# Rounding float64 weights on chip: the sign carried by a parametric activation on ScalarE in place of an operation on VectorE

## The chip, the cores and the metric

The kernel runs on one core of one Trainium2 chip. The metric is the time of one execution on the device in microseconds (us), the median of several runs. The profile is of one execution, with times counted from the start of its span. Its engines are PE (TensorE, matmuls; PEld is the loading of their weights), DVE (VectorE), ACT (ScalarE), POOL (GpSimd) and SP (SyncE, which here only issues transfers).

## The reference, cut to what matters

A retention block, linear attention with a decay per head, is followed by a SwiGLU feed-forward block. q, k and v are float32. The three weight matrices are float64, because `np.random.randn` gives float64 and nothing casts it.

```python
# attention: B, H, S, D = 8, 8, 576, 64
scores = scale * np.matmul(q, k.transpose(0, 1, 3, 2))
Dmat = np.where(rel >= 0, gamma[:, None, None] ** rel[None, :, :], 0.0)
attn = np.matmul(scores * Dmat[None], v).astype(np.float32)
x = attn.transpose(0, 2, 1, 3).reshape(B * S, H * D)          # 4608 x 512

# feed-forward: w_gate, w_val 512 x 1536, w_out 1536 x 512, all float64
g = x @ w_gate
silu = g * (1.0 / (1.0 + np.exp(-g)))
out = (silu * (x @ w_val) @ w_out).astype(np.float32)
```

[...]

## The kernel before: the parts that matter

The kernel works on the tokens in tiles. The first tile has 512 tokens and uses plain matmuls (`up0`, `down0`); while it runs, the weights arrive, are rounded, and sums of weight blocks are formed, which the later tiles of 1024 tokens use. Attention is woven in between: one `tick` moves three pairs of heads on by one stage each.

The weights come in 18 units of 1 MB, into a ring of three places. A unit has two halves of 128 x 512 numbers, and each half goes through `split` on ScalarE and then `rounding` on VectorE:

```python
def split(j):                                     # ScalarE
    i, f = halves[j]
    bits = bits_of(i, f)                          # 32-bit words of the float64 numbers: [..., 0] low, [..., 1] high
    top, ulp = [rest[:, part_at + 512 * (2 * n + j % 2) : ...] for n in range(2)]    # two places each, by j % 2
    nc.scalar.activation(out=blocks(top), in_=bits[:, :, :, 1].bitcast(F32), func=AF.Copy, scale=2.0 ** -112)
    nc.scalar.activation(out=blocks(ulp.bitcast(I32)), in_=bits[:, :, :, 0].bitcast(U32), func=AF.Copy, scale=2.0 ** -29)
    parts[j] = top.bitcast(I32), ulp.bitcast(I32)
    if f and j // 2 + RAWS < len(order):
        load_w(j // 2 + RAWS)                     # the next unit for this place of the ring

def rounding(j):                                  # VectorE
    i, f = halves[j]
    dst = weights[i][1][f].bitcast(I32)
    top, ulp = parts.pop(j)
    nc.vector.tensor_scalar(out=dst, in0=top, scalar1=3, scalar2=None, op0=ALU.logical_shift_left)       # L376
    nc.vector.scalar_tensor_tensor(out=top, in0=top, scalar=-(1 << 31), in1=dst,                         # L377
                                   op0=ALU.bitwise_and, op1=ALU.bitwise_or)
    nc.vector.tensor_tensor(out=dst, in0=top, in1=ulp, op=ALU.add)                                       # L379
    if j + 1 < len(halves):
        split(j + 1)
```

How this rounds: the high word of a float64 holds the sign, 11 bits of exponent and 20 of the fraction. Read as a float32, it has the sign, the upper 8 bits of that exponent in its own exponent field, and the other 3 bits, with the 20, in its fraction. The factor 2^-112 takes 112 from the exponent field. For the weights here what is left of the field is so small that a shift of the word by 3 to the left loses nothing of it, and the shifted word has just the exponent and the upper fraction of a float32. It does lose the sign, though, in bit 31; L377 takes that bit from `top` and puts it back. The low word, scaled by 2^-29 and rounded to an integer from 0 to 8, gives the last three bits of the fraction, and L379 adds it as an integer, with its carry.

The matmuls of the first tile:

```python
def up0(f, chunks):                               # f = 0 to 11
    pair = banks[2 * (f % 2) : 2 * (f % 2) + 2]   # bankA and bankB, or bankC and bankE
    for gv, bank in enumerate(pair):
        for c in chunks:
            nc.tensor.matmul(bank, w_up[...], xs[0][:, c, :], ...)                    # L567
    if HP - 1 in chunks:
        s = io[:, (f % 2) * T0 : (f % 2 + 1) * T0]
        nc.scalar.activation(out=s, in_=pair[0], func=AF.Silu)                        # L571
        nc.vector.tensor_tensor(out=hid0[f], in0=pair[1], in1=s, op=ALU.mult)         # L572, the product of f

down_order = [8, 9, 10, 0, 1, 11, 2, 3, 4, 5, 6, 7]
def down0(f):
    for i, bank in enumerate(banks):              # bankA, bankB, bankC, bankE
        nc.tensor.matmul(bank, hid0[f][:, ts(i, P)], w_dn[...], ...)                  # L579
```

The program of the first tile is one list, in which the halves to be rounded stand ahead of the matmuls that need them; each engine takes its instructions in that order. Other lines that the profile names:

- L403 to L414: transposes and scaling of q and k for attention (L410 on VectorE, L414 the scaling of keys on ScalarE)
- L426 to L462: attention's matmuls; L469 to L484: masks and states on VectorE, after ScalarE's copy `even` (L473); L511 and L513: attention's result into x
- L586: the first tile's output copied out of the banks
- L605: sums of blocks of x (VectorE), of weights and of hidden values (GpSimd, in part VectorE); L656: sums of `w_out` stored to memory, L283 to L290: the attention's loads, both on SP's queue
- L799 and L838: the matmuls of the later tiles; L740: sums of their results

Of the kernel before, what the change touches and what calls it, by code (L numbers as in the profile page):

```python
# [12 lines left out]
F32 = mybir.dt.float32  # L13
# [3 lines left out]
AF = mybir.ActivationFunctionType  # L17
ALU = mybir.AluOpType
# [131 lines left out]
def kernel(  # L150
# [32 lines left out]
    nc = tc.nc  # L183
# [21 lines left out]
    scale = 1.0 / math.sqrt(D)  # L205
# [131 lines left out]
    def load_w(m):  # L337
        i = order[m]
        raw = rest[:, raw_at + m % RAWS * 2048 : raw_at + (m % RAWS + 1) * 2048]
        raws[i] = raw.bitcast(I32)  # L340
        dst, src = raw.bitcast(I64), weights[i][0]
        if i < NUP:
            dst = dst.rearrange("p (c n) -> p c n", n=2 * P)
            for cols in (ts(0, P), ts(1, P)) if m == 0 else (slice(0, 2 * P),):
                nc.scalar.dma_start(out=dst[:, :, cols], in_=src[:, :, cols])
        else:
            nc.scalar.dma_start(out=dst.rearrange("p (f n) -> p f n", f=2), in_=src)

    def bits_of(i, f):

        if i < NUP:
            return raws[i].rearrange("p (c f m two) -> p f c m two", f=2, m=P, two=2)[:, f]
        return raws[i].rearrange("p (f c m two) -> p f c m two", f=2, m=P, two=2)[:, f]

    def split(j):

        i, f = halves[j]
        bits = bits_of(i, f)  # L360
        top, ulp = [rest[:, part_at + 512 * (2 * n + j % 2) : part_at + 512 * (2 * n + j % 2 + 1)] for n in range(2)]
        blocks = lambda a: a.rearrange("p (c m) -> p c m", m=P)
        nc.scalar.activation(out=blocks(top), in_=bits[:, :, :, 1].bitcast(F32), func=AF.Copy, scale=2.0 ** -112)
        nc.scalar.activation(out=blocks(ulp.bitcast(I32)), in_=bits[:, :, :, 0].bitcast(U32), func=AF.Copy, scale=2.0 ** -29)
        parts[j] = top.bitcast(I32), ulp.bitcast(I32)
        if f and j // 2 + RAWS < len(order):
            load_w(j // 2 + RAWS)

    def rounding(j):

        i, f = halves[j]
        dst = weights[i][1][f].bitcast(I32)
        top, ulp = parts.pop(j)
        nc.vector.tensor_scalar(out=dst, in0=top, scalar1=3, scalar2=None, op0=ALU.logical_shift_left)  # L376
        nc.vector.scalar_tensor_tensor(out=top, in0=top, scalar=-(1 << 31), in1=dst,  # L377
                                       op0=ALU.bitwise_and, op1=ALU.bitwise_or)
        nc.vector.tensor_tensor(out=dst, in0=top, in1=ulp, op=ALU.add)  # L379
        if j + 1 < len(halves):  # L380
            split(j + 1)

# [482 lines left out]
    for t in range(HP + 2):  # L865
        tick(t, 0, HP)
        if t == 2:
            split(0)
        if t in (2, 3, 4):
            for j in range(2):  # L870
                rounding(2 * (t - 2) + j)
        if t > 3:
            for f in range(2):
                up0(f, range(2) if t == 4 else range(2, HP))
# [14 lines left out]
    def round_until(i):  # L889
        while todo and order.index(i) >= todo[0]:  # L890
            m = todo.pop(0)
            plan.extend(lambda j=j: rounding(j) for j in (2 * m, 2 * m + 1))
# [92 lines left out]
```

## Time and profile before

| what | value |
|---|---|
| time, median of 3 runs | 1091.46 us (1091.33 to 1092.53) |
| span of the profiled execution | 1084.0 us |
| mean granted clock of TensorE | 0.994 |
| VectorE busy | 670.9 us, 62% |
| L376, shift: 36 instructions | 0.42 us each at the median |
| L377, sign: 36 instructions | 0.69 us each at the median |
| L379, add: 24 into `arena`, 12 into `rest` | 0.69 and 0.85 us each at the median |
| L363, ScalarE's Copy of the high words: 36 | 0.68 us each at the median |
| L364, ScalarE's Copy of the low words: 36 | 0.67 us each at the median |
| first and last instruction of the rounding | L363 at 27.5 us, L379 at 144.2 us |

How to read what follows. A row of the timeline has the start in us, the duration in us, engine, line, operation, output<-input with their shapes, the number of instructions, and in brackets how long the engine had been idle before and what released it. A row of groups has line, engine, operation, names and shapes and a count; then busy us and mean ns of one; then the idle time ahead of them. A row of stretches has the stretch from:to, its length, the busy us of each engine with the number of instructions, the granted clock of TensorE (1.00 is full), the mean busy share of the 16 DMA engines and GB/s. Some hundredths of overlap between instructions of one engine are usual[...].

### The profile page before, as it was taken

How to read it: one execution, taken by the hardware profiler on the slowest of the kernel's cores; microseconds unless marked ns; L12 is line 12 of the kernel's file. 1: busy time of each engine (PE TensorE's matmuls, PEld its weight loads, DVE VectorE, ACT ScalarE, POOL GpSimd, SP SyncE). 2: the span in 40 equal slices, each digit the busy share in tenths (PEclk: the TensorE clock that was granted, in tenths of full speed). 3: DMA queues.
4: the chain of work that ended last, by engine and by line, in shares of the span. 5: the costliest groups of instructions: out<-in, count | busy, mean ns of one | idle time of the engine just before them, and what ended most of it. 6: DMA issues, size and time to landing. Idle time of an engine off the chain costs nothing.

```text
span 1084.0 us, 21445 instructions
## 1 busy us (share of the span) xinstructions
PE 1047.0 (97%) x8420; PEld 859.6 (79%) x8420; DVE 670.9 (62%) x1063; ACT 267.5 (25%) x560; POOL 407.4 (38%) x357
## 2 busy tenths in 40 slices
PE   5899989999999899999999999999999999999998
PEld 4545445688888788888888888888888888888887
DVE  1699975976878867653646858535267464244644
ACT  3555511224232211222222111122211012231110
POOL 1002479566454403741216025622151375122504
PEclk9999999999999999999999999999999999999999
DMA  9989876656577878867657778554554555555653
GB/s 216 235 222 242 231 185 196 194 179 191 155 190 187 248 193 223 215 175 196 150 167 215 179 203 221 154 152 133 154 172 154 160 175 153 151 153 155 185 165 98
DMA packets 304212, 198.44 MB, mean 183 GB/s; under 512 B 219632, under 2 KB 247408, under 8 KB 304112
## 3 DMA queue, kind: packets, MB, share of 16 engines
q1 hardware_dynamic: 272512, 152.67, 54.3%
q10 hardware_dynamic: 31600, 44.41, 12.3%
q8 instruction: 67, 1.10, 0.4%
q14 instruction: 33, 0.27, 0.1%
HBM read 156.91 MB, written 40.11 MB: 182 GB/s over the span
## 4 chain that ended last, share of the span: by engine, by line
PE 79%; DVE 10%; DMA 4%; issue 3%; SPq 2%; POOL 2%; ACT 1%; ACTq 0%; DVEq 0%; POOLq 0%
PE bankA L799 11%; PE bankE L799 11%; PE bankB L799 11%; PE bankC L799 11%; PE bankE L838 6%; PE bankB L838 6%; PE bankC L838 6%; PE bankA L838 6%; PE outer L449 2%; DVE rest L740 2%; PE outer L426 1%; DVE rest L377 1%; DVE rest L605 1%; PE inner L462 1%; DMA v<-in_v_dram 1%
## 5 line engine op out<-in xcount | busy, mean ns | idle before, releaser
L740 POOL TENSOR_TENSOR rest<-rest 128x512 f32<-128x512 f32 x56 | 79.1, 1418 | 300.7 <-DVE rest L740 280.0
L814 ACT ACTIVATE io<-rest 128x256 f32<-128x256 f32 x180 | 75.0, 417 | 348.9 <-DVE rest L740 300.5
L799 PE MATMUL bankA<-rest,arena 128*128 128x256 f32 x544 | 130.5, 383 | 3.5 <-DVE rest L586 2.5
L799 PE MATMUL bankC<-rest,arena 128*128 128x256 f32 x544 | 129.3, 381 | 1.5 <-DVE rest L740 1.4
L605 POOL TENSOR_TENSOR rest<-rest 128x256 f32<-128x256 f32 (+1 forms) x86 | 83.6, 993 | 119.7 <-DVE rest L379 91.8
L605 POOL TENSOR_TENSOR arena<-arena 128x512 f32<-128x512 f32 (+1 forms) x72 | 115.2, 1614 | 32.6 <-DMA up<-arena 26.5
L799 PE MATMUL bankB<-rest,arena 128*128 128x256 f32 x512 | 121.9, 381 | 0.9 <-DVE arena L817 0.8
L799 PE MATMUL bankE<-rest,arena 128*128 128x256 f32 x512 | 121.4, 380 | 0.1
L799 PEld LDWEIGHTS bankA<-rest,arena 128*128 128x128 f32 x544 | 103.6, 191 | 19.8 <-issue 5.0
L799 PEld LDWEIGHTS bankC<-rest,arena 128*128 128x128 f32 x544 | 102.8, 190 | 16.8 <-issue 2.6
L821 POOL TENSOR_TENSOR arena<-rest,io 128x256 f32<-128x256 f32 x72 | 51.8, 726 | 168.8 <-ACT io L814 168.8
L799 PEld LDWEIGHTS bankB<-rest,arena 128*128 128x128 f32 x512 | 97.3, 191 | 15.4 <-DVE arena L817 1.2
L799 PEld LDWEIGHTS bankE<-rest,arena 128*128 128x128 f32 x512 | 96.9, 190 | 13.7 <-issue 0.4
L740 DVE TENSOR_TENSOR rest<-bankC,rest 128x512 f32<-128x512 f32 x72 | 48.9, 688 | 68.9 <-PE bankC L799 46.7
L740 DVE TENSOR_TENSOR rest<-bankE,rest 128x512 f32<-128x512 f32 x72 | 48.8, 686 | 67.5 <-PE bankE L799 49.3
L740 DVE TENSOR_TENSOR rest<-bankA,rest 128x512 f32<-128x512 f32 x72 | 48.8, 686 | 65.4 <-PE bankA L799 48.0
L740 DVE TENSOR_TENSOR rest<-bankB,rest 128x512 f32<-128x512 f32 x72 | 48.9, 687 | 62.6 <-PE bankB L799 46.3
L817 DVE SCALAR_TENSOR_TENSOR arena<-rest,io 128x256 f32<-128x256 f32 x84 | 53.8, 645 | 12.6 <-ACT io L814 12.6
L838 PE MATMUL bankB<-arena 128*128 128x256 f32 x252 | 58.2, 381 | 0.0
L838 PE MATMUL bankA<-arena 128*128 128x256 f32 x252 | 58.1, 380 | 0.0
L838 PE MATMUL bankC<-arena 128*128 128x256 f32 x252 | 58.0, 380 | 0.0
L838 PE MATMUL bankE<-arena 128*128 128x256 f32 x252 | 57.9, 380 | 0.0
(150 smaller groups left out, 1648.5 us busy)
## 6 DMA issues: line engine op xcount, KB each, us to landing
arena<-up SPq DMA_DIRECT2D x234, 256.0 KB, 2.7
arena<-dn SPq DMA_DIRECT2D x104, 384.0 KB, 3.6
up<-arena ACTq DMA_DIRECT2D x78, 256.0 KB, 2.8
out_dram<-rest SPq DMA_DIRECT2D x32, 256.0 KB, 3.3
qk<-in_q_dram SPq DMA_DIRECT2D x112, 72.0 KB, 3.3
qk<-in_k_dram SPq DMA_DIRECT2D x112, 72.0 KB, 2.9
v<-in_v_dram SPq DMA_DIRECT2D x62, 128.0 KB, 3.1
kn<-in_k_dram SPq DMA_DIRECT2D x58, 128.0 KB, 2.9
```

Source lines behind the costliest of these rows:

```text
L377: nc.vector.scalar_tensor_tensor(out=top, in0=top, scalar=-(1 << 31), in1=dst, op0=ALU.bitwise_and, op1=ALU.bitwise_or)
L426: m = nc.tensor.matmul(xo[half[hl], c, r], s["v"][half[r], c, hl, :], ret[half[r], hl, c], start=(c == 0), stop=(c == 0), skip_group_check ...
L449: nc.tensor.matmul(xr[half[hl]] if c + 1 == NC else xo[half[hl], c // 2, c % 2], state[half[hl], c, :], s["qT"][half[hl], ts(c, L)], start ...
L462: nc.tensor.matmul(sc[half[r], hl, c], kT[half[hl], at], qT[half[hl], at], start=True, stop=True, skip_group_check=True)
L605: eng.tensor_tensor(out=dst, in0=srcs[0], in1=srcs[1], op=ALU.add if op[0] == "add" else ALU.subtract)
L740: eng.tensor_tensor(out=at(op[1]), in0=at(op[2]), in1=at(op[3]), op=ALU.add if op[0] == "add" else ALU.subtract)
L799: nc.tensor.matmul(b[:, gv * TB : (gv + 1) * TB], w[:, gv, ts(c, P)], rhs[:, c, :], start=(opens and gv == 0 and c == 0), stop=(c == 1), s ...
L814: nc.scalar.activation(out=s, in_=src[:, 0:TB], func=AF.Silu, scale=-1.0 if negative else 1.0)
L817: return lambda: nc.vector.scalar_tensor_tensor(out=dst, in0=src[:, TB : 2 * TB], scalar=-1.0, in1=s, op0=ALU.mult, op1=ALU.mult)
L821: nc.gpsimd.tensor_tensor(out=dst, in0=src[:, TB : 2 * TB], in1=s, op=ALU.mult)
L838: nc.tensor.matmul(b[:, m * TB : (m + 1) * TB], lhs[:, qd, ts(m, P)], w[:, qd], start=(opens and qd == 0 and m == 0), stop=(qd == NQ - 1), ...
```

## The change

What is computed stays the same. The high word's activation becomes a parametric one: it multiplies by `scale` as before, and values below zero also by `alpha`, 2^32. That adds 32 to the exponent field of negative numbers, which is bit 28 of the word; the shift by 3 takes this bit to bit 31, where the sign belongs. VectorE's operation that put the sign back (L377) is then not needed, and the add works on the shifted word in place. Its aim is less work for VectorE.

```diff
-        nc.scalar.activation(out=blocks(top), in_=bits[:, :, :, 1].bitcast(F32), func=AF.Copy, scale=2.0 ** -112)
+        nc.scalar.activation(out=blocks(top), in_=bits[:, :, :, 1].bitcast(F32), func=AF.Prelu, scale=2.0 ** -112, alpha=2.0 ** 32)
         nc.scalar.activation(out=blocks(ulp.bitcast(I32)), in_=bits[:, :, :, 0].bitcast(U32), func=AF.Copy, scale=2.0 ** -29)
...
         nc.vector.tensor_scalar(out=dst, in0=top, scalar1=3, scalar2=None, op0=ALU.logical_shift_left)
-        nc.vector.scalar_tensor_tensor(out=top, in0=top, scalar=-(1 << 31), in1=dst,
-                                       op0=ALU.bitwise_and, op1=ALU.bitwise_or)
-        nc.vector.tensor_tensor(out=dst, in0=top, in1=ulp, op=ALU.add)
+        nc.vector.tensor_tensor(out=dst, in0=dst, in1=ulp, op=ALU.add)
```

## The prediction

> **What bounds the kernel now.** The page's first part comes first. It makes TensorE the bound of the whole span:
>
> ```profile
> PE 1047.0 (97%) x8420; PEld 859.6 (79%) x8420; DVE 670.9 (62%) x1063; ACT 267.5 (25%) x560; POOL 407.4 (38%) x357
> ```
>
> Such a share is an average, so I next placed the removed line in time. L377 runs 36 times, from 28.7 to 144.1 us, and nowhere later. So I cut the span at the places where the work changes and asked for busy times in those stretches. The columns are stretch, length, then busy us and instructions of PE, PEld, DVE, ACT and POOL, then clock, DMA share and GB/s.
>
> ```profile
> 26.00:37.00 11.00, 7.94 (x263) 7.50 (x263) 9.40 (x23) 7.02 (x15) 0.00 (x0) 0.85 1.01 242
> 37.00:116.00 79.00, 78.81 (x602) 38.43 (x590) 67.11 (x127) 39.77 (x71) 7.04 (x7) 1.00 0.96 232
> 116.00:151.00 35.00, 28.77 (x319) 15.13 (x320) 32.60 (x52) 13.45 (x26) 18.94 (x21) 0.95 0.73 198
> 151.00:187.00 36.00, 35.82 (x535) 20.38 (x534) 17.27 (x36) 3.98 (x9) 34.85 (x49) 1.00 0.69 201
> 187.00:205.00 18.00, 15.52 (x41) 8.70 (x40) 17.80 (x22) 1.68 (x4) 10.39 (x9) 0.91 0.49 149
> ```
>
> Most of the rounding lies in 37 to 116, and there TensorE is idle for 0.2 us of 79 at full clock. A faster VectorE can win nothing in it directly. From 116 to 151 it is the other way round: VectorE is busy 93% of the stretch, TensorE is idle for 6.23 us. The timeline of TensorE names these waits (the bracket is idle time before the row and its releaser):
>
> ```profile
> 117.16 3.70 PE L567 MATMUL bankA<-rest,arena 128*128 128x512 f32 x8 [1.18 <-ACT io L571]
> 135.50 0.69 PE L426 MATMUL outer<-ret,v 64*64 64x64 f32 x32 [1.10 <-DVE ret_last L477]
> 138.15 1.15 PE L449 MATMUL outer<-qT,state 64*64 64x64 f32 x32 [1.26 <-DVE state L484]
> 139.50 0.27 PE L456 MATMUL outer<-qT,kT 64*64 64x64 f32 x2 [0.20 <-DVE kT L410]
> 145.51 2.08 PE L579 MATMUL bankE<-rest,arena 128*128 128x512 f32 x2 [2.44 <-DVE arena L572]
> 147.38 1.77 PE L579 MATMUL bankA<-rest,arena 128*128 128x512 f32 x2
> ```
>
> The reader is to see that five waits add up to 6.18 us and that all come from a late VectorE. The first names ScalarE, but its SiLU at 116.52 stands behind two splits (115.40, 115.97) which had waited for VectorE's rounding. And the last wait leaves the clock low: two groups of L579 start 1.87 and 1.60 us apart, against 0.86 later, 1.75 us lost.
>
> How late VectorE is, its own timeline shows:
>
> ```profile
> 128.12 0.68 DVE L572 TENSOR_TENSOR arena<-bankE,io 128x512 f32<-128x512 f32 x1
> 144.77 0.68 DVE L572 TENSOR_TENSOR arena<-bankE,io 128x512 f32<-128x512 f32 x1
> ```
>
> These are the products of f = 9 and f = 11. TensorE had finished their bankE at 116.0 and 134.4, so VectorE is 12 and 10 us behind, without idle time of its own.
>
> [...] The trace [...] shows Copy, 0.66 us, and SiLU, 0.59 us, of 512 elements each close together; no run before has a Prelu. [...] L377 takes 0.69 us alone and up to 1.11 us while GpSimd is busy. [...] here a wait of 2.44 us was enough for a slow stretch, one of 1.26 us was not.
>
> **The change part by part.** The groups by form of VectorE from 28 to 145 us give the prices (busy us, mean ns, idle before):
>
> ```profile
> L379 DVE CUSTOM_DVE_ANT_0 arena<-rest 128x1024 uint16<-128x1024 uint16 x24 | 17.7, 738 | 2.3
> L377 DVE SCALAR_TENSOR_TENSOR rest<-rest,arena 128x512 int32<-128x512 int32 x24 | 16.7, 695 | 0.8
> L377 DVE SCALAR_TENSOR_TENSOR rest<-rest 128x512 int32<-128x512 int32 x12 | 10.4, 863 | 0.4
> L376 DVE TENSOR_SCALAR arena<-rest 128x512 int32<-128x512 int32 x24 | 10.1, 422 | 0.7 <-ACT rest L363 0.7
> ```
>
> *Removed:* 36 instructions of L377, 16.7 + 10.4 = 27.1 us of VectorE, and 0.03 us of gap each, 28 us in all. Of this, 25 of the 36 fall into 37 to 116, beside a dense TensorE.
>
> *Added:* nothing by count. The order of instructions on all five engines is otherwise the same, and both programs have two table loads[...]. I take Prelu at Copy's 0.68 us.
>
> *Moved:* the add reads the shifted word in place and now waits for the shift itself. `top` is free after the shift, one instruction earlier than before; ScalarE's second activation gets a wait of its own for the buffer of `ulp`, released by the add.
>
> *The new pace of a half.* Before, a half comes every 1.79 or 1.89 us when nothing disturbs (54.52, 56.31, 58.20). Less 0.73 (0.69 and the start gap), that is 1.06 to 1.16. ScalarE's two activations start 0.59 and 0.58 apart: 1.17 us a half. So both engines run at about 1.17, ScalarE just the slower: a gain of about 0.65 a half inside a run of halves.
>
> *Replay of VectorE.* I kept the order and let each product wait for its bank. From 91.2: four halves to 95.9, product f = 6, two halves, f = 7 at 100 (its bankE is full at 99.3), the attention pieces to 106.6, four halves to 111.3, f = 8 at 111.9 (117.49 before), four halves, f = 9 at about 117 (128.12 before). The backlog is gone, and from there the products follow the banks. f = 11 comes just after TensorE ends it.
>
> *Replay of TensorE.* It stays dense from 37 on. Without the five waits it reaches L579's first bank at 136.2 instead of 140.2 and then runs through: 6.18 us of waits and 1.75 us of low clock, 7.9 us.
>
> *Ahead of 37:* the wait of 2.68 us at 34.0 for L477 stands behind ScalarE's copy `even` (32.69), and ScalarE there is held by its copies and a DMA issue, not by L377. I give 0.1 us.
>
> *After 151:* TensorE is dense to 196.9, so all that follows should move ahead by the same 8 us. Sum: 8.0 us. I put 0.5 more for the stretch at 187 to 205 (below): 1091.5 - 8.5 = 1083.0.
>
> **The rivals.** (1) *All of VectorE's time returns*: 28 us off, 1063. The chain that ended last speaks for it, as it runs over L377 from 91 to 143; against it, TensorE is dense beside the first 25 of the 36. Unlikely. (2) *Transfers take the place of the wait.* The weights come as 1 MB loads in a ring of three, 5.7 to 6.8 us to land, and DMA is at 0.96 in 37 to 116. If VectorE gets ahead, the loads of the fifth and third last pair may come 1 or 2 us late. For it: little headroom. Against: nearly no split waited for weights before, and the replay has several us of slack ahead of each product's use. If it bites, the gain is 3 to 5: 1087. (3) *GpSimd does not move along.* Its sums are dense from 150.4 to 197.5, after stores queued behind the attention's loads. If these loads stay where they are, TensorE meets the sums at 199 earlier than GpSimd is ready, and 3 to 6 us come back: 1087. For moving along: the load ahead of those stores was issued at 139.47, right as VectorE's transpose ended at 139.38, so it comes forward with VectorE. (4) *More than 8.* From 187 to 199 VectorE's additions take 1.1 to 1.75 us instead of 0.69 beside GpSimd, and TensorE waits 2.48 us for the copy of bankA, then runs slowly (1.75 us). If GpSimd is done sooner, up to 4 more: 1079. (5) *Prelu dearer than Copy*: each 0.1 us would add 3.6 us to ScalarE, which is busy half of the time; nearly harmless.
>
> **Range and chances.** The waits of 6.2 us are named one by one and I trust them. The low clock, the stretch at 187 to 205, and (2) and (3) add about 4 us to either side: 1079 to 1088.5. A gain of 2% would need 21.8 us, of which only rival 1 is capable; a loss of 2% would need an effect that neither the order nor the trace shows.
>
> **What the profile after must show.** 36 fewer VectorE instructions, its busy time near 644; Prelu at 0.66 to 0.70 us; two table loads. TensorE idle under 1 us from 116 to 145, the first L579 near 136, no slow pair there; the product of f = 9 near 117. The first L799 near 191.5. The prediction is wrong if TensorE's idle time comes back with a DMA or GpSimd as releaser, if Prelu costs clearly more, or if the low clock shows up elsewhere.

## The result, and the profile after

Measured side by side, the kernel before took 1091.39 us and the changed one 1086.33 us (medians of four runs each). The ratio is 0.9956 with a 95% interval of 0.9937 to 0.9976, about 5 us or 0.4% less. A second comparison of the same two programs, with 22 and 51 runs, gave 0.9992 (0.9979 to 1.0006), which is no difference. Executions of either program are spread over some 8 to 10 us (the 51 runs of before from 1085.2 to 1093.2), so a few runs decide little here. The two intervals, put in us, are a gain of 2.6 to 6.9 and of -0.7 to 2.3; they don't overlap, so I claim no more than a gain between nothing and 5 us, where 8.5 had been predicted. For the mechanism I rely on the traces, and on experiments that moved the time by 11 to 14 us.

The first part of the page of after, in the form of the row shown of before:

```profile
PE 1046.6 (96%) x8420; PEld 861.8 (79%) x8420; DVE 642.2 (59%) x1027; ACT 267.4 (25%) x560; POOL 402.0 (37%) x357
```

VectorE has 36 instructions and 28.7 us of work less, and TensorE's share has not grown. Where VectorE's time went, the same stretches tell (stretch, length, then busy us and instructions of PE, PEld, DVE, ACT and POOL, then clock, DMA share, GB/s), here of after:

```profile
26.00:37.00 11.00, 6.48 (x218) 5.85 (x209) 7.62 (x20) 7.55 (x16) 0.00 (x0) 0.91 0.97 239
37.00:116.00 79.00, 78.82 (x618) 39.54 (x616) 53.52 (x107) 41.71 (x74) 5.95 (x7) 0.99 0.96 241
116.00:151.00 35.00, 35.00 (x470) 19.36 (x470) 20.73 (x40) 10.95 (x21) 16.03 (x21) 1.00 0.72 182
151.00:187.00 36.00, 30.45 (x388) 17.44 (x387) 16.64 (x33) 3.98 (x9) 34.84 (x49) 0.91 0.68 200
187.00:205.00 18.00, 15.44 (x50) 8.99 (x49) 17.79 (x22) 2.08 (x5) 10.28 (x9) 1.00 0.49 152
```

From 116 to 151 TensorE is busy for 35.00 of 35 us, where it had been for 28.77: the stretch that the change was meant for is repaired, and its clock is at 1.00. But from 151 to 187, which was dense before, TensorE is now busy for 30.45 of 36 us at a clock of 0.91. What was won in the one stretch is lost in the next. The rows with a wait in TensorE's timeline from 130 to 200 us name the waits (idle time before the row and its releaser in brackets):

```profile
156.64 0.70 PE L425 MATMUL outer<-ret,v 64*64 64x64 f32 x32 [3.13 <-DVE ret_last L476]
160.25 1.97 PE L448 MATMUL outer<-qT,state 64*64 64x64 f32 x32 [2.24 <-DVE state L483]
185.14 0.33 PE L444 MATMUL outer<-ret_last,vl 64*64 64x64 f32 x4 [0.18 <-PE outer L425]
199.46 1.97 PE L798 MATMUL bankA<-rest,arena 128*128 128x256 f32 x8 [2.56 <-DVE rest L585]
```

(Behind the rounding a line of after has a number one lower than the same line of before; L363, L364 and L376 of before, the splits and the shift, are L364, L365 and L377 of after, and its L378 is the add.) Between 130 and 153 us there is no wait at all. The last group of L578 ahead of the two waits comes 8.00 us before the same group of the kernel before (after, then before):

```profile
152.49 1.02 PE L578 MATMUL bankE<-rest,arena 128*128 128x512 f32 x2
```

```profile
160.49 1.02 PE L579 MATMUL bankE<-rest,arena 128*128 128x512 f32 x2
```

Then attention's matmuls wait 3.13 and 2.24 us for VectorE's masks and states, and at 164.94 the lead is down to 0.18 us (the same group of before starts at 165.12). The later tiles' first matmul, L798, begins at 199.46. Before it began at 199.57:

```profile
199.57 3.27 PE L799 MATMUL bankA<-rest,arena 128*128 128x256 f32 x8 [2.48 <-DVE rest L586]
```

VectorE isn't late of itself now. Its own timeline and that of ScalarE, both of after, lead on to the cause:

```profile
155.77 0.69 DVE L468 TENSOR_TENSOR ret<-inner,near 128x512 f32<-128x512 f32 x1 [8.86 <-ACT even L472]
```

```profile
153.53 1.71 ACTq L655 DMA_DIRECT2D dn<-rest  x3
155.36 0.37 ACT L472 COPY even<-inner 128x256 f32<-128x256 f32 x1 [17.42 <-DMA dn<-rest]
165.88 0.37 ACT L472 COPY even<-inner 128x256 f32<-128x256 f32 x1 [9.34 <-DMA dn<-rest]
```

The mask L468 waits 8.86 us for ScalarE's copy `even`. TensorE had finished the copy's input at 146.4, but ScalarE reaches it only after three stores of `w_out` sums (L655) that stand ahead of it in its order. The third row is the next tick's. The chain of waits that ended last runs over the same places: GpSimd's sums at 150.36 and 153.47, ScalarE's store at 154.22, `even` at 155.36, L468 at 155.77, the state at 159.23, and TensorE's L448 at 160.25.

ScalarE issues 24 of the 78 stores of these sums; not all are on SP's queue, as the list of lines said. The other 54 and attention's loads share the queue of SP, of which these are some rows in after:

```profile
113.88 11.63 SPq L655 DMA_DIRECT2D dn<-rest  x9
125.61 2.08 SPq L283 DMA_DIRECT2D qk<-in_q_dram  x4
133.88 5.48 SPq L655 DMA_DIRECT2D dn<-rest  x9
139.45 2.09 SPq L283 DMA_DIRECT2D qk<-in_q_dram  x4
147.83 3.96 SPq L655 DMA_DIRECT2D dn<-rest  x8
```

and the same queue in before, where these three rows answer to the last three:

```profile
133.69 5.43 SPq L656 DMA_DIRECT2D dn<-rest  x9
139.47 2.76 SPq L283 DMA_DIRECT2D qk<-in_q_dram  x4
147.91 3.96 SPq L656 DMA_DIRECT2D dn<-rest  x8
```

The starts agree within 0.2 us, although VectorE was 10 us behind in the one kernel and not in the other. So close an agreement is in part chance: in second executions, described below, the three rows start at 135.84, 141.60 and 150.56 (before) and at 133.97, 140.19 and 149.22 (after). But neither execution of after has them some 8 us earlier, so from here on this chain of sums, stores and loads doesn't follow the rounding. In before it couldn't be seen. There the copy `even` came at nearly the same time, after ScalarE had been idle for 14.20 us, and TensorE had nothing to wait for because it reached the tick's first matmul only at 161.44 (timeline of ScalarE in before):

```profile
155.79 0.38 ACT L473 COPY even<-inner 128x256 f32<-128x256 f32 x1 [14.20 <-POOL rest L605]
```

GpSimd, at last, waits for the stores to free the places of its sums (timeline of GpSimd in after):

```profile
117.65 1.88 POOL L604 TENSOR_TENSOR rest<-rest 128x256 f32<-128x256 f32 x2 [16.95 <-DMA dn<-rest]
135.92 0.72 POOL L604 TENSOR_TENSOR rest<-rest 128x256 f32<-128x256 f32 x1 [6.38 <-DMA dn<-rest]
150.36 1.40 POOL L604 TENSOR_TENSOR rest<-rest 128x256 f32<-128x256 f32 x2 [6.98 <-DMA dn<-rest]
196.27 1.17 POOL L604 TENSOR_TENSOR rest<-rest 128x256 f32<-128x256 f32 x1
```

A store waits for a sum, a sum waits for an earlier store, and the loads of attention stand between them in the same queue. The last of these sums ends at 197.4 in after and at 197.6 in before, and the later tiles' first matmul follows about 2 us behind it. It isn't released by GpSimd, though, but by VectorE's copy L585 at 198.63, which stands behind VectorE's own sums of x. These begin at 187.24 (187.43 in before), right after attention's last result, and take up to 1.75 us each beside GpSimd, where the ones after 198 take 0.69.

### The profile page after: what moved, and what is told of

Read it like the earlier page. It is cut to its first block, busy times and chain, and to the rows that moved or that the text cites. A ratio compares the mean times of both kernels' runs of the same rounds, so it can differ in the third digit from the quotient of the medians.

```text
span 1084.9 us, 21409 instructions
## 1 busy us (share of the span) xinstructions
PE 1046.6 (96%) x8420; PEld 861.8 (79%) x8420; DVE 642.2 (59%) x1027; ACT 267.4 (25%) x560; POOL 402.0 (37%) x357
## 4 chain that ended last, share of the span: by engine, by line
PE 82%; DVE 8%; DMA 4%; issue 2%; POOL 2%; SPq 1%; ACT 1%; ACTq 0%; DVEq 0%; POOLq 0%
PE bankE L798 10%; PE bankC L798 10%; PE bankA L798 10%; PE bankB L798 10%; PE bankE L837 6%; PE bankB L837 6%; PE bankA L837 6%; PE bankC L837 6%; PE outer L448 3%; PE bankA L566 2%; PE bankC L566 2%; DVE rest L739 2%; PE bankE L566 2%; PE bankB L566 2%; DVE rest L604 2%
## 5 line engine op out<-in xcount | busy, mean ns | idle before, releaser
L798 PE MATMUL bankA<-rest,arena 128*128 128x256 f32 x544 | 129.1, 380 | 3.6 <-DVE rest L585 2.6
L798 PE MATMUL bankC<-rest,arena 128*128 128x256 f32 x544 | 129.3, 381 | 2.5 <-DVE rest L739 1.4
L604 POOL TENSOR_TENSOR rest<-rest 128x256 f32<-128x256 f32 (+1 forms) x86 | 80.6, 958 | 124.7 <-DMA kn<-in_k_dram 89.5
L798 PE MATMUL bankE<-rest,arena 128*128 128x256 f32 x512 | 122.8, 383 | 0.0
L798 PE MATMUL bankB<-rest,arena 128*128 128x256 f32 x512 | 121.9, 381 | 0.9 <-DVE arena L816 0.8
L798 PEld LDWEIGHTS bankA<-rest,arena 128*128 128x128 f32 x544 | 103.1, 190 | 19.2 <-issue 5.0
L798 PEld LDWEIGHTS bankC<-rest,arena 128*128 128x128 f32 x544 | 102.9, 190 | 17.8 <-issue 2.6
L798 PEld LDWEIGHTS bankB<-rest,arena 128*128 128x128 f32 x512 | 97.5, 191 | 15.2 <-DVE arena L816 1.2
L798 PEld LDWEIGHTS bankE<-rest,arena 128*128 128x128 f32 x512 | 97.8, 192 | 14.0 <-DVE rest L739 0.4
```

Source lines behind the costliest of these rows:

```text
L604: eng.tensor_tensor(out=dst, in0=srcs[0], in1=srcs[1], op=ALU.add if op[0] == "add" else ALU.subtract)
L798: nc.tensor.matmul(b[:, gv * TB : (gv + 1) * TB], w[:, gv, ts(c, P)], rhs[:, c, :], start=(opens and gv == 0 and c == 0), stop=(c == 1), s ...
```

## The experiments

The theory to be tested: **a second limit stood right behind the first**, namely the sums on GpSimd together with their stores in the queues of SP and ScalarE, and it didn't move with VectorE. Rivals: the parametric activation costs something; the whole difference is chance between executions; the waits at 156 and 160 come only from ScalarE's order, without GpSimd; attention's transfers are late by themselves. Each kernel was compared with the kernel before on the same chip, and ratios are to that kernel.

| kernel | median us | ratio (95%) |
|---|---|---|
| c1_control: before, unchanged | 1091.10 | 1.0002 (0.9987 to 1.0017) |
| c4_prelu_only: before, with Prelu, sign kept | 1090.65 | 1.0003 (0.9989 to 1.0017) |
| c2_after_free: after, `even` and keys on VectorE | 1092.36 | 1.0012 (0.9996 to 1.0028) |
| c3_before_free: before, the same move | 1092.01 | 1.0024 (1.0011 to 1.0038) |
| d1_after_again: after, unchanged | 1089.06 | 0.9992 (0.9979 to 1.0006) |
| d2_after_ready: after, stores wait for no sum | 1074.77 | 0.9870 (0.9852 to 0.9888) |
| d3_before_ready: before, the same | 1087.93 | 0.9994 (0.9981 to 1.0007) |
| d4_after_first: after, first nine stores on ScalarE | 1086.28 | 0.9980 (0.9969 to 0.9991) |
| e1_after_even: after, only `even` on VectorE | 1089.04 | 0.9997 (0.9983 to 1.0011) |
| e2_after_first_even: the last two together | 1086.78 | 0.9972 (0.9960 to 0.9985) |
| e3_after_acts_even: all 26 stores on ScalarE, and `even` | 1083.71 | 0.9939 (0.9917 to 0.9961) |
| e4_after_pool: after, the 26 stores issued by GpSimd | 1078.08 | 0.9894 (0.9874 to 0.9913) |

### How much is chance

**c1_control** is the kernel before, with no edit.

> The kernel before, unchanged, as a control and for a second profile of it. Theory A (the 8 us won at 116 to 151 us are real, and most of them are given back from 151 to 163 us, where ScalarE's copy `even` stands behind stores that wait for GpSimd): ratio 1.000 +- 0.002; the second profile again shows TensorE idle for about 6 us between 116 and 151 us and dense from 151 to 187. Rival C (the first profile of before, at a span of 1084.0 us, was a short execution, and only the tail after 199 us differs between executions): the first L799 again at about 199.5, and the rest longer by some us.

The ratio is 1.0002. Its profile again has five waits from 116 to 151 us, 6.07 us in all (four of them in the same places as before; the fifth, 0.49 us, is at bankB instead of attention's L426), and L799 begins at 198.51, but then TensorE waits five times between 205 and 221 us, 3.7 us in all, which the first profile of before doesn't show. The profile of before was of a short execution (span 1084.0, against 1086.2 in the control; by the metric 1085.71 us, 5.8 below the median of its runs). Part of what the spans of single profiles differ by comes from there, so I compare starts ahead of 200 us rather than spans.

**d1_after_again** is the changed kernel, with no edit.

> The changed kernel once more, for a firmer ratio and a second profile. All theories: ratio 0.996 +- 0.002; TensorE dense from 116 to about 153, then waits of some 5 us between 153 and 163.

The ratio is 0.9992. TensorE is busy for 35.00 of 35 us from 116 to 151 again, and the waits after it are larger than in the first profile of after (timeline of TensorE):

```profile
158.13 1.13 PE L425 MATMUL outer<-ret,v 64*64 64x64 f32 x32 [5.21 <-DVE ret_last L476]
200.84 3.59 PE L798 MATMUL bankA<-rest,arena 128*128 128x256 f32 x8 [2.19 <-DVE rest L585]
```

Here L798 begins 1.3 us later than in before, and its first group takes 3.59 us after the wait. The same group took 3.27 us in before, at a granted clock of 0.58, and 1.97 us in after, at 1.00. Both executions show the stretch repaired and its gain gone by 200 us.

### Does Prelu cost anything

**c4_prelu_only** takes the new activation into the kernel before and keeps the operation for the sign:

```diff
-        nc.scalar.activation(out=blocks(top), ..., func=AF.Copy, scale=2.0 ** -112)
+        nc.scalar.activation(out=blocks(top), ..., func=AF.Prelu, scale=2.0 ** -112, alpha=2.0 ** 32)
```

> The kernel before with Prelu in place of Copy, and the sign operation kept (the result is the same). All theories: Prelu costs ScalarE what Copy does (0.67 us), VectorE is as late as before; ratio 1.000 +- 0.002. If Prelu had a cost of its own, 36 of them would show as more than 2 us.

The ratio is 1.0003: nothing. The instruction itself took 0.674 us at the median in after, Copy 0.682 in before, and ScalarE is busy for 267.8 us of the first 1084 in this run, where it was for 267.5 in before. This rival is out.

### A first attempt at the second limit, and a mistake

**c2_after_free** and **c3_before_free** let VectorE do the copy `even` and the scaling of keys in ticks 10 to 12, so that no attention work stands behind the stores on ScalarE:

```diff
         def keys():
             for hl in range(2):
+                if 10 <= i <= 12:
+                    nc.vector.tensor_scalar(out=kn[:, :, hl, :], in0=kn[:, :, hl, :], scalar1=key[...], scalar2=None, op0=ALU.mult)
+                    continue
...
-            nc.scalar.copy(out=even, in_=z[:, 0])
+            if 10 <= i + 1 <= 12:
+                nc.vector.tensor_copy(out=even, in_=z[:, 0])
+            else:
+                nc.scalar.copy(out=even, in_=z[:, 0])
```

> The changed kernel, and for the ticks 10 to 12 the copy `even` and the scaling of keys are on VectorE in place of ScalarE, whose queue holds the stores of GpSimd's sums. Theory A: the two waits of TensorE at 156.6 (3.13 us) and 160.3 (2.24 us) and the slow clock behind them are gone, TensorE is dense from 116 to about 189, the first L798 comes near 192 to 194 in place of 199.5, and the time falls by a further 4 to 7 us against the changed kernel: near 1080, ratio to before about 0.989. Rival B (attention's load number 10, or the sums themselves, are what is late, and not ScalarE's order): TensorE waits at 153 to 160 as before, now for VectorE which waits for a transfer; time as the changed kernel, 1086. Rival D (what is won ahead of 199 is given back at 199 to 220, where TensorE meets GpSimd's sums too early): dense to 189, but then waits for GpSimd of about the same size; 1086.

> The kernel before with the same move of ticks 10 to 12 to VectorE. Theory A: VectorE's backlog up to 145 us is the limit there and ScalarE's order is not, so nothing is gained: ratio 1.000 +- 0.002, or 1 us slower by the extra work on VectorE. If the move alone is worth 4 us or more here, theory A is wrong on the two limits standing one behind the other.

Neither is faster: the ratios are 1.0012 and 1.0024. Theory A's 1080 us for the first is far off, and the second is some 2.6 us slower, a little more than expected. The copy no longer waits for a store, but the scaling of keys took a wait with it into VectorE's order (timelines of VectorE, TensorE and SP's queue in c2_after_free):

```profile
175.89 0.54 DVE L414 TENSOR_SCALAR kn<-kn,tab 128x256 f32<-128x256 f32 x1 [19.04 <-DMA kn<-in_k_dram]
```

```profile
178.73 1.14 PE L429 MATMUL outer<-ret,v 64*64 64x64 f32 x32 [11.89 <-DVE ret_last L483]
```

```profile
171.82 1.13 SPq L264 DMA_DIRECT2D kn<-in_k_dram  x2
```

The keys' load is issued only at 171.82 (166.65 in after). Ahead of it in SP's queue stand eight loads of q and k, which waited 15.7 us in all for earlier stores of sums. VectorE stood still for the keys for 19 us, with all that followed. So the run doesn't test what I meant it to. It does show that SP's queue is late as well, not only ScalarE's order.

### Taking the wait for the sums away

**d2_after_ready** and **d3_before_ready** leave GpSimd's sums in place, but let each store of a `w_out` sum read a block that has long been rounded. The stores have the same size, queue and order, and wait for no sum; no sum waits for a store to have read its place, either. The later tiles compute with other weights because of this, so the kernel computes something else there; the amount of work is the same.

```diff
                 src, queue = view(slot), nc.scalar if late else nc.sync
+                src = w_dn[:, qd, 0, 0]
```

> The changed kernel; every store of a sum of w_out takes its data from a block that was rounded long ago in place of GpSimd's sum (the same bytes from the same queues in the same order; the later tiles then compute with other weights). So no store waits for GpSimd, and no sum waits for a store to have read its place. Theory A2 (the chain of GpSimd's sums, their stores in SP's and ScalarE's queues, and the attention's loads and ScalarE's work that stand behind these stores, runs at its own pace and ends the stretch from 153 to 187): TensorE dense from 116 to about 188, the first L799 near 190 to 194 in place of 199.5, time 5 to 8 us below the changed kernel: 1079 to 1081. Rival B2 (attention's transfers themselves are late, whatever stands ahead of them): waits of TensorE for masks or keys of 4 us or more remain between 150 and 180, time as the changed kernel.

> The kernel before with the same stores of ready data. Theory A2: VectorE's backlog still ends the stretch up to 145, the first L579 stays near 140 with the waits of 6 us ahead of 146; 151 to 187 was dense already, so the gain is at most what contention at 187 to 205 gives, 0 to 4 us: 1087 to 1091. A gain of 5 us or more here would mean that the stores and not VectorE's sign operation were the limit of the kernel before.

With the change, this takes 1074.77 us, a ratio of 0.987; without it, 1087.93 us, a ratio of 0.9994. This is the clearest result, and the gain is larger than theory A2's 5 to 8 us. Neither the change nor ready stores alone is worth a measurable gain in these runs (0.9992 and 0.9994), but both together are worth 1.3%, about 14 us. The stretches from 151 on in d2_after_ready:

```profile
151.00:187.00 36.00, 35.82 (x406) 19.13 (x405) 19.17 (x35) 2.81 (x6) 16.79 (x20) 1.00 0.85 238
187.00:205.00 18.00, 17.90 (x81) 15.11 (x80) 17.55 (x24) 6.59 (x13) 8.71 (x6) 1.00 0.88 247
```

TensorE is dense through both, and its first matmul of the later tiles begins 11.85 us earlier than in after (timeline of TensorE, then of ScalarE):

```profile
187.61 1.89 PE L799 MATMUL bankA<-rest,arena 128*128 128x256 f32 x8
```

```profile
145.24 0.37 ACT L472 COPY even<-inner 128x256 f32<-128x256 f32 x1 [8.61 <-PE inner L461]
```

The copy `even`, at 155.36 in after, no longer waits for a store but for TensorE. Attention's loads hardly started earlier: in after those at 125.61, 139.45 and 151.89, here at 124.13, 139.36 and 153.93; only the last one's keys left clearly earlier, at 161.12 and not 166.65. So the second limit lies in what waits for a sum or a store, not in the start of these loads, and this is against rival B2.

In d3_before_ready the first limit is still there, and late VectorE makes TensorE wait as late as 152.93 us:

```profile
124.87 5.82 PE L567 MATMUL bankA<-rest,arena 128*128 128x512 f32 x8 [5.68 <-ACT io L571]
152.93 1.97 PE L579 MATMUL bankE<-rest,arena 128*128 128x512 f32 x2 [2.57 <-DVE arena L572]
```

The wait at 124.87 was 1.18 us in before: its SiLU stands behind splits that wait for VectorE. So the edit also made VectorE later, and the 0.9994 isn't the worth of ready stores with the first limit left as it was. VectorE works beside a busier GpSimd there (27.4 us from 116 to 151, against 18.9 in before), and its 47 instructions of that stretch take 33.46 us, where 52 took 32.60 in before; that this is the reason wasn't tried. The wait ahead of the later tiles' first matmul, 2.48 us in before, is gone in this run; that matmul comes at 204.39.

### Which queue has to be relieved

Five more kernels keep all the arithmetic and change only where a store is issued, or where `even` is copied.

**d4_after_first** lets ScalarE issue the first nine of the 26 stores, which come after f = 7:

```diff
-                plan.append(lambda ..., late=f + 1 == NF: group(late))
+                plan.append(lambda ..., late=f in (7, NF - 1): group(late))
```

> The changed kernel, with the first nine stores of sums (those of f = 7) issued by ScalarE in place of SP, where they stand behind the attention's load 8 and GpSimd waits 17 us for them (100.7 to 117.7). The result is the same. Theory A2: GpSimd's sums, the stores after them and the loads 9 to 11 all come forward by 5 to 10 us, the waits of TensorE at 153 to 163 shrink or go, time 3 to 7 us below the changed kernel: 1080 to 1083. Rival B2: the loads are paced by the weights' transfers up to 120 us and come forward little; 1086. Rival E: ScalarE's splits now wait behind the stores, VectorE gets late again; 1087 to 1090.

The ratio is 0.998. The waits at 155 and 159 are 1.53 and 2.25 us (3.13 and 2.24 in after), and L798 begins at 198.01, 1.5 us earlier than in after: a small part of the loss, and less than the 3 to 7 us expected (the changed kernel had 0.9992 in this comparison). Only the first of the three loads came forward much, from 125.61 to 114.94; the others came 3.6 and 1.6 us earlier.

**e1_after_even** moves only `even` to VectorE, as in c2, and leaves the keys on ScalarE.

> The changed kernel, with the copy `even` of ticks 10 to 12 on VectorE and the scaling of keys left on ScalarE. The result is the same. Theory A3 (after d2: the stores that wait for GpSimd's sums hold both ScalarE's `even` and, in SP's queue, the attention's load 11): the waits of TensorE near 156 for the masks shrink to under 2 us, but the keys of tick 11, loaded late, stop it near 170 by some us; first L799 near 197 to 199, time 0 to 3 us below the changed kernel. Rival F (only ScalarE's order holds TensorE): TensorE dense to 189, time 6 us or more below the changed kernel.

The ratio is 0.9997. The wait for the masks is gone, and the keys take its place, since they stand behind the same stores (TensorE, then ScalarE):

```profile
156.85 1.42 PE L434 MATMUL inner<-v,kn 64*64 64x64 f32 x29 [4.70 <-ACT kn L413]
```

```profile
156.29 0.51 ACT L413 ACTIVATE kn<-kn,tab 128x256 f32<-128x256 f32 x1 [20.33 <-DMA dn<-rest]
```

So moving single pieces of work out of ScalarE's order didn't help here. This is against the rival that held ScalarE's order alone responsible.

**e2_after_first_even** has both edits.

> The changed kernel with both: `even` of ticks 10 to 12 on VectorE, and the first nine stores issued by ScalarE. The result is the same. Theory A3: sums and load 11 some us earlier, so 3 to 6 us below the changed kernel, ratio to before 0.994 to 0.997. Rival F: no more than e1.

The ratio is 0.9972, about 3 us. The later tiles begin at 192.84, 6.6 us earlier than in after. But the three stores of the output that stand ahead of ScalarE's part of the first tile's output (L590) then take 6.22 us to issue, against 1.62 in after; L590 comes at 201.58, released by a store of a sum, and TensorE waits for it (timeline of TensorE):

```profile
202.31 3.61 PE L801 MATMUL bankE<-rest,arena 128*128 128x256 f32 x8 [4.05 <-ACT rest L590]
```

**e3_after_acts_even** has all 26 of these stores on ScalarE, with `even` on VectorE, so that SP's queue holds only loads there:

```diff
-                plan.append(lambda group=groups.pop(0)[1], late=f + 1 == NF: group(late))
+                plan.append(lambda group=groups.pop(0)[1]: group(True))
```

> As e2, but all stores of the sums of the first quarter of w_out (26) are issued by ScalarE, so that SP's queue has only the attention's loads up to load 11. The result is the same. Theory A3: loads 9 to 11 come forward by 5 us or more; if ScalarE's splits don't fall behind, 4 to 8 us below the changed kernel. Rival E (ScalarE's splits and SiLU fall behind the stores): TensorE waits for ScalarE between 100 and 140, time as the changed kernel or above.

The ratio is 0.9939. TensorE is dense from 151 to 205 us, but ahead of that ScalarE stands for 14.74 us behind eleven stores before a split of weights at 127.60; the SiLU that follows begins only at 132.90, and TensorE waits for it, as rival E had it (timeline of TensorE):

```profile
133.53 6.29 PE L569 MATMUL bankC<-rest,arena 128*128 128x512 f32 x8 [7.80 <-ACT io L573]
```

**e4_after_pool** lets GpSimd issue the 26 stores itself, right after the sums that they store. No other engine then stands behind one of these 26 sums; the stores of later sums stay on SP and ScalarE.

```diff
-                src, queue = view(slot), nc.scalar if late else nc.sync
+                src, queue = view(slot), nc.gpsimd if qd == 0 else nc.scalar if late else nc.sync
```

> The changed kernel, with those 26 stores issued by GpSimd itself. The result is the same. Theory A3: no queue of another engine waits for these sums, SP's loads 9 to 11 come forward, TensorE's waits at 153 to 163 shrink; each issue costs GpSimd time, and [...] its sums end 0 to 10 us later or earlier than at 197; time 1 to 6 us below the changed kernel. Rival G (GpSimd's time for the issues exceeds what its waits were): sums end after 205, TensorE waits for them there, time above the changed kernel.

It takes 1078.08 us, a ratio of 0.9894 (0.9874 to 0.9913), 11.2 us less than before, and more than the 1 to 6 us below the changed kernel that were expected. The changed kernel wasn't part of this comparison; its own ratios were 0.9956 and 0.9992. Its six runs lie within 1.6 us. Its stretches:

```profile
116.00:151.00 35.00, 34.88 (x469) 19.10 (x468) 30.29 (x52) 14.15 (x28) 31.22 (x45) 1.00 0.78 210
151.00:187.00 36.00, 35.82 (x406) 19.14 (x405) 19.86 (x34) 2.81 (x6) 34.03 (x44) 1.00 0.65 190
```

TensorE is dense in both. GpSimd is busy for 31.2 us of the first, of which 9.65 us are the issuing of 17 stores; so 21.6 us are work on sums, where it had been 16.0. From 99 to 152 us its longest wait for a store to free a place is 0.73 us, against 16.95 in after. Its last sum and TensorE's start of the later tiles come 10.7 and 8.7 us earlier than in after:

```profile
185.62 1.17 POOL L604 TENSOR_TENSOR rest<-rest 128x256 f32<-128x256 f32 x1
```

```profile
190.74 1.96 PE L798 MATMUL bankA<-rest,arena 128*128 128x256 f32 x8 [0.47 <-DVE rest L585]
```

The price is GpSimd's own time for issuing (groups by tile; min, median and max in ns):

```profile
L655 POOL DMA_DIRECT2D dn<-rest x26: 539/562/777, 99.2 to 140.0; - x26
```

That is 0.56 us each and some 15 us in all, and ahead of 19 of the issues GpSimd stands for about 0.30 us more, 5.7 us in all. This comes out of time in which it had been idle. `even`, at 155.36 in after, comes at 147.74, released by TensorE and not by a store, and the load of the next keys leaves at 158.95 instead of 166.65.

## Why the prediction was right, and where it was not

The measured 1086.33 us lies in the range of 1079 to 1088.5, and within 2% of before, as predicted. But it lies 3.3 us above the predicted value, and that it lies in the range is in part luck: the repeated comparison's ratio of 0.9992, taken from 1091.39 us, would be 1090.5, outside of it. The mechanism was right up to 153 us and wrong from there. Two of the prediction's own signs of being wrong appeared: the low clock showed up elsewhere, and TensorE's idle time came back, with VectorE as its releaser but ScalarE's copy and a store behind it.

- **VectorE's work.** Predicted 36 instructions fewer and 644 us; measured 36 fewer and 642.2. The time per half also came out: predicted 1.17 us, and the shifts L377 start at 56.87, 58.03 and 59.20.
- **Prelu at Copy's price.** Predicted 0.66 to 0.70 us, measured 0.674. That was an estimate from Copy (0.66) and SiLU (0.59) in the trace of before, in which no Prelu runs. The number of table loads stayed at two, of 1.28 us each, and ScalarE has 560 instructions in both kernels: no further load and no extra instruction for negatives.
- **The five waits of 116 to 151.** Predicted to go entirely, with the low clock behind them; measured 35.00 busy us of 35 at full clock. The first L578 began at 136.6 (predicted near 136). The product of f = 11 came at 134.04. The lead of 8.00 us at 152.49 agrees with the predicted 8.0, but this too is partly luck: this execution began the first `up0` 1.29 us later than before (38.70 against 37.41), so the stretch gave 9.3 us. In d1_after_again the lead at the same group is 8.60, begun 0.57 late, so 9.2. The sum of waits and low clock, 7.9, was thus 1.3 to 1.4 us short. The 136.2 in the prediction's replay has a slip as well: only four of the five waits, 3.74 us, stand ahead of L579, which gives 136.5.
- **The product of f = 9** came at 120.56, not near 117. VectorE waits now and then for ScalarE's split there, 1.28 us at 117.12 for example; that split had itself stood for 2.39 us, released by a transfer. That is near to rival (2), in small; it costs TensorE nothing.
- **The step that failed** is "After 151 TensorE is dense to 196.9, so all that follows should move ahead by the same 8 us". TensorE was dense there before *because* it came late. The copy `even`, which its matmuls at 153.4 needed, came at 155.79 in before and at 155.36 in after. Of the lead of 8.00 us, 7.82 are gone at 164.94: 5.37 us in the two waits (3.13 and 2.24), and most of the rest in groups at a low clock behind the second one (0.50 from 160.25 to 162.25 and 0.54 from there to 165), L448 for 1.97 us, L461 for 1.11 and L578 for 1.88, where the same groups took 1.11, 0.65 and 1.12 in before.
- **The argument behind it**, under rival (3), was that a load was issued at 139.47, right as VectorE's transpose ended at 139.38, and would come forward with VectorE. (139.38 is the start of the next instruction; the transpose ended at 139.45.) That was a coincidence: the stores ahead of the load had been issued only at 139.12. In after the transposes end at 131.7 and the load still leaves at 139.45, right behind nine stores that stand ahead of it from 133.88 on, some of which wait for GpSimd. So rival (3) was right that GpSimd's chain would not move along, but wrong on where it would be met: not at 199 by the sums themselves, but at 153 to 163 through ScalarE's copy, and 7.8 us came back, not 3 to 6. d2_after_ready and e4_after_pool show that this chain is the cause, as each removes its waits in another way and has the later tiles begin at 187.61 and 190.74, where "near 191.5" had been predicted.
- **The half microsecond at 187 to 205** did not come: TensorE is busy there for 15.44 us, against 15.52.

What stays open: where the 1.3 to 1.4 us come from that the stretch up to 153 gave beyond the sum; why the two comparisons of the same pair differ by more than their intervals suggest; what decides, from one execution to another, whether TensorE waits between 205 and 221 us; and why a load of attention waits for earlier stores even where its turn in the queue has come (in after SP stands for 5.0 us ahead of the load at 161.44, released by a store). None of these was tried by itself.

## What to carry to other kernels

Before you sum up what a removed wait is worth, ask of every later stage what else would be ready by the new, earlier time: a dense stretch behind a wait tells only that the other engines were no later than the bound, not that they could be earlier. A chain that keeps its absolute times although the engine that was sped up comes earlier, as the stores at 133.7 and 133.9 here, is a candidate for the next limit; as such starts differed by 2 us between executions of one kernel, only an experiment decides. And a store that waited for a slow producer held up here what stood behind it in the order of the engine that issues it (`even` came at 155.36, 9 us after its input was ready). With the 26 stores issued by their producer, the same copy came at 147.74 and waited for TensorE and not for a store, and this made the difference between 0 to 5 us and 11 us here.

## What was not expected of the hardware

A store issued by GpSimd took it 0.56 us of its own time in e4_after_pool, against 0.40 us on SP and 0.38 on ScalarE for stores of the same size in after; even with the 0.30 us ahead of most of them this was little enough to pay. And the length of a wait didn't by itself decide, as the prediction took it to, whether the clock was low behind it. The wait of 2.44 us in before was followed by a group at half speed (2.08 us at a granted clock of 0.50), but the one of 3.13 us in after by L425 for 0.70 us, at a clock of 1.00 (156.60 to 157.40). In d1_after_again the groups were slow behind the wait of 5.21 us (L425 for 1.13 us) and still slow behind the next one, of 1.32 us (L448 for 1.97, where it took 1.11 in before). In c1_control a wait longer than the 2.44 us was followed by a group at full speed, in a stretch with a clock of 1.00:

```profile
147.50 1.13 PE L579 MATMUL bankE<-rest,arena 128*128 128x512 f32 x2 [2.76 <-DVE arena L572]
```
